# Windowed and pooled attention with a dense layer behind it: the first two dense tiles move into the banks that pair 0 leaves, with the planner's tables set anew

## The chip, the core and the metric

The kernel runs on one core of a Trainium2 chip. The core has a matrix engine (TensorE, PE in the profile), three engines for elementwise work (VectorE or DVE, ScalarE or ACT, GpSimd or POOL) and SyncE (SP), which issues the DMAs. Each engine works through its own queue in order and waits for others by semaphores. The metric is the device time of one execution in microseconds; the median of eight runs stands for a kernel.

## What is computed

Attention in two forms over q, k and v of 8 batches, 8 heads, 576 positions and 64 channels, and a dense layer on their sum:

```python
q_d, k_d, v_d = mean of 4 neighbouring positions of q, k, v
out_up = np.repeat(softmax(q_d k_d.T / 8) v_d, 4, axis=positions)
mask = np.abs(pos[:, None] - pos[None, :]) < 4
out_local = softmax(where(mask, q k.T / 8, -1e9)) v
x = (out_up + out_local)            # 4608 tokens x 512
h = x @ w_in                        # 512 x 2048
out = (h - np.tanh(h)) @ w_out      # 2048 x 512
```

## The kernel before

**Units.** Two heads are a pair (32 pairs), two pairs a group (16 groups), four pairs a batch. For a group, q and k come in by DMA as float32 (`qkn`), are cast and sorted to bfloat16 (`reorder`, L491), transposed by TensorE (`turn`, L520) and copied from PSUM into `qk` in two halves or as a whole (L529). Two adds (L533 into `half`, L538 into `qkd`) make the pooled q and k. v is cast (`prep_v`, L443), and its pooled form made by TensorE (`pool_v`, L462 and L464) and copied out (L469).

**A pair** (`attention`): scores of four windows (L587, for the first four pairs on top of a bias matmul, L581), their exponential (L623), the fifth window and the pooled scores (L587, L606) with theirs (L649, L652), the products with v (L669, L675), a reciprocal (L686), the normalisation into `ln` (L688), and the way back to channels on partitions. That way is either transposes (L744 to L748) with a copy `od` (L751) and an add (L754), or, for pairs in the table `UP`, "up" matmuls that add the repeated pooled part in PSUM (L723, L728) with one or two copies into `xT` (L734). From pair 12 on it is a DMA transpose.

**Dense layer.** The tokens are taken in 9 blocks of 512. `mm1` makes one tile of h (128 features by 512 tokens) from four matmuls, one for each chunk of 128 input channels. Chunk j is the `xT` of pair j of the batch, so block 0 needs pairs 0 to 3. Then come tanh on ScalarE (L786) and the subtraction on VectorE (L789); `mm2` makes the output from 16 matmuls for each 128 tokens. These 1,152 matmuls, 128x512, are most of TensorE's work, and are put between the steps of later pairs.

**PSUM.** There are eight banks. `ps_ts` and `ps_ox` (two banks each) serve attention throughout. `ps_ts1` and `ps_ox1` serve pairs 0 and 2 of the first batch only (pair 2 has its outputs in `ps_ts1`). Then `dense_banks` closes their pool and opens one of four dense banks, `ps_hy`. Tiles 0 to 3 of `mm1` therefore list both old names, "ts1" and "ox1", as written: they come after everything in these banks.

**Order.** The order is not written out. Steps are recorded with an engine (or a list of engines to choose from), a cost in ns, what they read and write, and a priority. `Program.order` then plays a greedy schedule through: on every engine the ready step of smallest priority goes first, and of steps with a choice the engine that is free first takes it. What comes out is each engine's fixed queue. Where the plan leaves TensorE idle before the dense layer, `emit` puts in filler matmuls (L1064). Tables give single steps their choice: `RE`, `RS` (sort), `TU`, `TS` (copies after the transposes; `TS` parts them in two halves), `AD`, `AS` (the adds; `AS` parts them), `CV` (v casts), `VD` (pooled v), `UP`, `PV` and `PLACE` (when a step is recorded), `URG` and `LATE` (priorities).

**What the steps of the prediction touch.** In the first 30 us: group 0's q and k (L491, L529, L533, L538), the pooled v of groups 0 and 1 (L469), the outputs and `ln` of pairs 0 to 3, their `xT` copies (L734), the casts of w_in (L434), and the first `mm1` tiles (L777). Later: pair 6's way back, and group 5's copies near 75 us.

Of the kernel before, what the change touches and what calls it, by code (L numbers as in the profile page):

```python
# [8 lines left out]
FP32 = mybir.dt.float32  # L9
# [3 lines left out]
PSUM = bass.MemoryType.PSUM  # L13


class Program:
# [147 lines left out]
def kernel(  # L164
# [26 lines left out]
    N_DC = Dm // 128  # L191
# [28 lines left out]
    vd = fixed("vd", [128, 2, 4, 65], BF16, NVW)  # L220
# [8 lines left out]
    od = fixed("od", [128, G], BF16, 2)  # L229
# [33 lines left out]
    op = P.op  # L263
# [497 lines left out]
    hy = [0]  # L761
    un = [0]

    def mm1(kb, fc):
        slot, us, g = hy[0] % 4, un[0] % 3, kb % 2
        hy[0] += 1
        un[0] += 1
        bs = sorted({kb * 512 // S, (kb * 512 + 511) // S})

        cut = 3 if kb == 0 and fc < 4 else 2  # L770
        old = ["ts1", "ox1"] if kb == 0 and fc < 4 else []

        def mm(part):
            if not ps_hy:
                dense_banks()
            for dc in range(cut) if part == 0 else range(cut, N_DC):
                T.matmul(ps_hy[slot], w_in_sb[:, dc, fc * 128:(fc + 1) * 128],  # L777
                         xT[dc][:, kb * 512:kb * 512 + 512],
                         start=(dc == 0), stop=(dc == N_DC - 1))
        for part in range(2):  # L780
            dcs = range(cut) if part == 0 else range(cut, N_DC)
            op("PE", 216 * len(dcs), lambda part=part: mm(part),
               reads=[("w_in", fc // 4, c) for c in dcs] +
               [(name, b, j) for b in bs for j in dcs for name in ("x", "xh")],
               writes=[("hy", slot)] + old, pri=P_A if old and part == 0 else 5000)
# [65 lines left out]
    def dense(kb):  # L851
# [18 lines left out]
        if kb == NBLK:  # L870
# [14 lines left out]
    T_QK, T_V, T_W, W_PRI = 900, 780, 2750, 53  # L885
    CAST = [("POOL", 620, GP.tensor_copy), ("ACT", 620, A.copy),
# [4 lines left out]
    CV = {0: 3, 1: 0, 2: 0, 3: 3, 4: 0, 5: 0, 6: 3, 7: 1, 8: 2, 9: 0, 10: 1, 11: 3}  # L891
# [4 lines left out]
    RE = {(0, 0): 0, (0, 1): 0, (1, 0): 1, (1, 1): 1, (2, 0): 1, (2, 1): 0, (3, 0): 3, (3,  # L896
          1): 0, (4, 0): 2, (4, 1): 1, (5, 0): 0, (5, 1): 0}
# [3 lines left out]
    TU = {(0, 0): 0, (0, 1): 0, (1, 0): 2, (1, 1): 2, (2, 0): 0, (2, 1): 0, (3, 0): 2, (3,  # L901
          1): 0, (4, 0): 0, (4, 1): 1, (5, 0): 1, (5, 1): 0}
# [12 lines left out]
    half_v, half_p = ("DVE", 420, 260, V), ("POOL", 650, 500, GP)  # L915
# [7 lines left out]
    URG = {'e1': {4: -2, 5: -2, 6: -2, 7: -2, 8: -2, 9: -2, 10: -2, 11: -2}, 'e2': {0: -2,  # L923
          1: -2, 2: -2, 3: -2, 4: -2, 5: -2, 6: -2, 7: -2, 8: -2, 9: -2, 10: -2, 11: -2},
          'norm': {0: -2, 1: -2, 2: -2, 3: -2, 4: -2, 5: -2, 6: -2, 7: -2}, 'add': {0: -2,
          1: -2}, 'turn': {4: -2, 5: -2}, 'vd': {4: -2, 5: -2}}
    ADDERS = [[("DVE", 760, 440, V), ("POOL", 1190, 850, GP)],
              [("POOL", 1190, 880, GP)], [("DVE", 760, 440, V)]]
    AD = {(0, 0): 1, (0, 1): 0, (1, 0): 0, (1, 1): 1, (2, 0): 1, (2, 1): 0, (3, 0): 0, (3,
          1): 1, (4, 0): 0, (4, 1): 0, (5, 0): 0, (5, 1): 2}  # L930
# [8 lines left out]
    for i in range(2):  # L939
        def guards(i=i):  # L940
# [3 lines left out]
           writes=[("qk", i, a, y) for a in range(2) for y in range(2)])  # L944
    for i in range(NVW):
        def ones(i=i):
# [3 lines left out]
           writes=[("vd", i), ("vw", i, 0), ("vw", i, 1)])  # L950
# [3 lines left out]
           writes=[("vd", i)], pri=-96)  # L954
# [141 lines left out]
```

The softmax here doesn't subtract the row's maximum and nothing guards it: scores larger than these inputs give would overflow.

## Time and profile before

| | us |
|---|---|
| median of 8 runs (lowest, highest) | 335.48 (334.74, 336.36) |
| the profiled execution | 335.51 |
| its span, first to last instruction | 333.8 |
| TensorE busy | 319.9 |
| VectorE, ScalarE, GpSimd busy | 236.5, 209.6, 155.5 |
| dense matmuls of line 777, mean of one | 0.379 |
| normalisation (L688), mean of one | 1.089 |
| granted TensorE clock over the span | 0.999 |

The profile is one execution. A matmul's busy time includes its passage through the array, so that following matmuls overlap: dense ones start every 0.215 us, although one lasts 0.379. A line of the timeline gives start, length, engine, source line, operation, output and inputs, shapes, count, and in brackets how long the engine had been idle and who ended that.

### The profile page before, as it was taken

How to read it: one execution, taken by the hardware profiler on the slowest of the kernel's cores; microseconds unless marked ns; L12 is line 12 of the kernel's file. 1: busy time of each engine (PE TensorE's matmuls, PEld its weight loads, DVE VectorE, ACT ScalarE, POOL GpSimd, SP SyncE). 2: the span in 40 equal slices, each digit the busy share in tenths (PEclk: the TensorE clock that was granted, in tenths of full speed). 3: DMA queues.
4: the chain of work that ended last, by engine and by line, in shares of the span. 5: the costliest groups of instructions: out<-in, count | busy, mean ns of one | idle time of the engine just before them, and what ended most of it. 6: DMA issues, size and time to landing. Idle time of an engine off the chain costs nothing.

```text
span 333.8 us, 6822 instructions
## 1 busy us (share of the span) xinstructions
PE 319.9 (96%) x2563; PEld 168.4 (50%) x2606; DVE 236.5 (71%) x386; ACT 209.6 (63%) x338; POOL 155.5 (47%) x183
## 2 busy tenths in 40 slices
PE   8778999999999999999999999999999999999996
PEld 5454555655554555554445444444444444444444
DVE  3697988789998879989687878787666443343300
ACT  1775877768858577668878786976654444444411
POOL 8673766249699488793939385652000000000000
PEclk9999999999999999999999999999999999999999
DMA  6999999999993889799899889843233000100012
GB/s 207 253 380 322 301 269 355 241 247 278 308 262 88 218 208 278 200 224 253 227 248 265 212 238 190 164 98 89 59 76 73 33 31 31 63 33 31 31 70 90
DMA packets 96878, 60.47 MB, mean 181 GB/s; under 512 B 74510, under 2 KB 80078, under 8 KB 96846
## 3 DMA queue, kind: packets, MB, share of 16 engines
q1 hardware_dynamic: 96846, 60.04, 67.0%
q8 instruction: 20, 0.33, 0.4%
q14 instruction: 12, 0.10, 0.1%
HBM read 43.05 MB, written 9.44 MB: 157 GB/s over the span
## 4 chain that ended last, share of the span: by engine, by line
PE 82%; DVE 9%; issue 4%; POOL 3%; ACT 1%; POOLq 0%; DVEq 0%; ACTq 0%
PE ps_hy L777 35%; PE ps_hy L832 34%; PE ps_ts L587 3%; PE ps_ox L669 3%; PE ps_ox L675 2%; DVE ln L688 2%; PE ps_ts L520 1%; DVE qk L529 1%; PE ps_hy L807 1%; DVE half L533 1%; DVE qr L491 1%; DVE E L656 1%; DVE gT L789 1%; DVE E L627 1%; DVE qkd L538 1%
## 5 line engine op out<-in xcount | busy, mean ns | idle before, releaser
L777 PE MATMUL ps_hy<-xT,w_in_sb 128*128 128x512 bf16 x553 | 141.8, 379 | 2.2 <-issue 1.1
L832 PE MATMUL ps_hy<-w_out_sb,gT 128*128 128x512 bf16 x540 | 137.2, 379 | 1.4 <-issue 0.5
L789 DVE TENSOR_TENSOR gT<-ps_hy,uy 128x512 bf16<-128x512 f32 x144 | 95.2, 685 | 57.9 <-ACT uy L786 56.1
L786 ACT ACTIVATE uy<-ps_hy 128x512 f32<-128x512 f32 x144 | 83.4, 601 | 61.6 <-PE ps_hy L777 57.3
L777 PEld LDWEIGHTS <-w_in_sb 128*128 128x128 bf16 x576 | 53.1, 98 | 59.3 <-issue 1.0
L832 PEld LDWEIGHTS <-gT 128*128 128x128 bf16 x560 | 52.3, 98 | 58.1
L533 POOL TENSOR_TENSOR half<-qk 128x576 f32<-128x576 bf16 (+1 forms) x33 | 34.9, 1061 | 39.1 <-ACT qk L529 34.6
L688 DVE TENSOR_TENSOR ln<-ps_ox,r 128x896 bf16<-128x896 f32 x30 | 32.7, 1089 | 0.8
L623 ACT ACTIVATE E<-ps_ts 128x960 bf16<-128x960 f32 x30 | 29.4, 981 | 2.1 <-PE ps_ts L587 2.1
L843 ACT COPY uy<-ps_hy 128x512 f32<-128x512 f32 x35 | 20.6, 589 | 14.3 <-PE ps_hy L832 12.6
L443 POOL CAST vw<-vst 128x640 bf16<-128x640 f32 x27 | 24.2, 900 | 10.7 <-DMA vst<-in_v_dram 7.3
L708 DVE TENSOR_TENSOR xT<-lnT 128x480 bf16<-128x480 bf16 (+1 forms) x40 | 28.2, 721 | 0.0
L356 POOL TENSOR_TENSOR qkn<-qkn 128x512 f32<-128x512 f32 (+1 forms) x18 | 25.1, 1397 | 4.9 <-DMA qkn<-in_v_dram 4.2
L529 ACT COPY qk<-ps_ts 128x1152 bf16<-128x1152 bf16 (+1 forms) x16 | 16.1, 1004 | 17.3 <-DVE qk L529 6.6
L627 DVE TENSOR_TENSOR E<-E,mask 128x960 bf16<-128x960 bf16 x28 | 23.3, 831 | 4.4 <-ACT E L623 4.4
L538 POOL TENSOR_TENSOR qkd<-half 128x288 bf16<-128x288 f32 (+1 forms) x31 | 20.9, 677 | 4.0 <-DVE half L533 2.7
L529 ACT COPY qk<-vst 128x1152 bf16<-128x1152 bf16 x10 | 22.1, 2209 | 0.9 <-POOL half L533 0.7
L491 DVE CAST qr<-qkn 128x1152 bf16<-128x1152 f32 (+1 forms) x18 | 17.8, 988 | 3.8 <-DMA qkn<-in_q_dram 2.3
L491 POOL CAST qr<-qkn 128x1152 bf16<-128x1152 f32 (+1 forms) x14 | 17.0, 1217 | 6.2 <-DMA qkn<-in_k_dram 3.2
L669 PEld LDWEIGHTS <-E 128*128 128x128 bf16 x300 | 15.3, 98 | 7.3 <-issue 0.6
L669 PE MATMUL ps_ox<-vw,E 128*128 128x65 bf16 x300 | 18.2, 194 | 0.5 <-DVE xT L734 0.3
L587 PEld LDWEIGHTS <-qk 64*128 64x128 bf16 x320 | 9.5, 95 | 17.6 <-issue 15.6
(107 smaller groups left out, 295.6 us busy)
## 6 DMA issues: line engine op xcount, KB each, us to landing
vst<-in_v_dram SPq DMA_DIRECT2D x62, 160.0 KB, 4.9
qkn<-in_q_dram SPq DMA_DIRECT2D x32, 288.0 KB, 4.3
qkn<-in_k_dram SPq DMA_DIRECT2D x32, 288.0 KB, 5.0
out_dram<-uy SPq DMA_DIRECT2D x35, 256.0 KB, 3.6
qkn<-in_v_dram SPq DMA_DIRECT2D x9, 512.0 KB, 5.1
gT<-in_moe_w_in_dram SPq DMA_DIRECT2D x4, 1024.0 KB, 9.2
xT<-in_moe_w_out_dram SPq DMA_DIRECT2D x8, 256.0 KB, 4.9
gT<-in_moe_w_out_dram SPq DMA_DIRECT2D x2, 1024.0 KB, 7.5
```

The costliest lines, as they stand in the source:

```text
L491: P.choice([(eng, ns, lambda fn=fn, x0=x0, x1=x1: fn(out=dst[:, x0:x1], in_=srt[:, x0:x1])) for eng, ns, fn in table], reads=[("qkn", sn, ...
L529: fn(out=o[:, ys].rearrange("p y (g a) -> p y g a", a=A6), in_=b16.rearrange("p (a g y) -> p y g a", a=A6, y=2)[:, ys])
L533: eng.tensor_tensor(out=half[:, ys], in0=four[:, ys, :, 0:2], in1=four[:, ys, :, 2:4], op=ALU.add)
L623: op("ACT", 980, lambda: A.activation(out=e1, in_=ps[:, :, 0:480], func=AF.Exp, scale=SCALE), reads=ts, writes=[("E", se, 0)], pri=URG.get ...
L627: op("DVE", 900, lambda: V.tensor_tensor(out=e1, in0=e1, in1=mask[:, 0:480].unsqueeze(1).to_broadcast([128, 2, 480]), op=ALU.mult), reads= ...
L669: T.matmul(po[:, hh, 65 * t:65 * t + 65], E[se][:, c:c + 128], vw[w][:, 2 * jj + hh, t, :], start=True, stop=True)
L688: op("DVE", 1090, lambda: V.tensor_tensor(out=ln[sl].rearrange("p n (h d) -> p h n d", d=D), in0=blocks[:, :, :, 0:64], in1=r[s].unsqueeze ...
L708: up=up: eng.tensor_tensor(out=xo[:, QW * t0:QW * t0 + nt * n].rearrange("p (t g a) -> p t g a", t=nt, a=4), in0=lnT[sl][:, t0:t0 + nt, 0: ...
L777: T.matmul(ps_hy[slot], w_in_sb[:, dc, fc * 128:(fc + 1) * 128], xT[dc][:, kb * 512:kb * 512 + 512], start=(dc == 0), stop=(dc == N_DC - 1))
L786: op("ACT", 490, lambda: A.activation(out=u[us], in_=ps_hy[slot], func=AF.Tanh), reads=[("hy", slot)], writes=[("u", us)], pri=-1)
L789: op("DVE", 620, lambda: V.tensor_tensor(out=gT[g][:, fc, :], in0=ps_hy[slot], in1=u[us], op=ALU.subtract), reads=[("hy", slot), ("u", us) ...
L832: T.matmul(ps_hy[slot], gT[g][:, fc, ts * 128:ts * 128 + 128], w_out_sb[:, fc, :], start=(fc == 0), stop=(fc == N_FF - 1))
```

## The change

The pool of `ps_ts1` and `ps_ox1` becomes two pools, one bank pair each, and `dense_banks(slot)` closes them one by one: first `ps_ox1` for dense banks 0 and 1, then `ps_ts1` for 2 and 3. Tiles 0 and 1 of `mm1` list only "ox1", tiles 2 and 3 only "ts1". Tiles 0 and 1 are recorded in three parts (chunks 0 and 1; 2; 3), tiles 2 and 3 in two (chunks 0 to 2; 3). The tables get new values.

```diff
-    early = ExitStack()
-    psum_e = early.enter_context(tc.tile_pool(name="psum_e", bufs=1, space=PSUM))
-    ps_ts1 = fixed("ps_ts1", [128, 2, 512], FP32, pool=psum_e)
-    ps_ox1 = fixed("ps_ox1", [128, 2, 512], FP32, pool=psum_e)
-
-    def dense_banks():
-        early.close()
-        pool = ctx.enter_context(tc.tile_pool(name="psum_d", bufs=1, space=PSUM))
-        ps_hy.extend(fixed("ps_hy", [128, 512], FP32, 4, pool=pool))
+    early = [ExitStack() for _ in range(2)]
+    pools = [s.enter_context(tc.tile_pool(name=f"psum_e{i}", bufs=1, space=PSUM,
+                                            side=("left", "right")[i]))
+             for i, s in enumerate(early)]
+    ps_ts1 = fixed("ps_ts1", [128, 2, 512], FP32, pool=pools[0])
+    ps_ox1 = fixed("ps_ox1", [128, 2, 512], FP32, pool=pools[1])
+    def dense_banks(slot):
+        while slot >= len(ps_hy):
+            i = len(ps_hy)
+            early.pop().close()
+            pool = ctx.enter_context(tc.tile_pool(name=f"psum_d{i}", bufs=1, space=PSUM,
+                                                  side=("right", "left")[i // 2]))
+            ps_hy.extend(fixed(f"ps_hy{i}", [128, 512], FP32, 2, pool=pool))
...
-        cut = 3 if kb == 0 and fc < 4 else 2
-        old = ["ts1", "ox1"] if kb == 0 and fc < 4 else []
+        old, parts = [], (range(0, 2), range(2, 4))
+        if kb == 0 and fc < 4:
+            old = ["ox1"] if fc < 2 else ["ts1"]
+            parts = (range(0, 2), range(2, 3), range(3, 4)) if fc < 2 else (range(3), range(3, 4))
...
-               writes=[("hy", slot)] + old, pri=P_A if old and part == 0 else 5000)
+               writes=[("hy", slot)] + old, pri=P_A if old and dcs[-1] < 3 else 5000)
...
-    P_A, LATE = 5000, {0: 25, 2: 40, 3: 40}
+    P_A, LATE = 5000, {0: 40, 2: 40, 3: 40}
...
-    PV = {2: 0, 3: 0, 4: -1, 5: -1, 6: 0}
-    PLACE = {2: (1, 3), 3: (1, 2), 4: (4, 4), 5: (1, 2), 6: (4, 4), 7: (1, 1), 8: (3, 3)}
+    PV = {2: 0, 3: 1, 4: -1, 5: 0, 6: 1}
+    PLACE = {2: (0, 2), 3: (1, 2), 4: (4, 4), 5: (1, 2), 6: (4, 4), 7: (1, 1), 8: (3, 3)}
...
-    PV1 = True
-    VD = {0: 1, 1: 2, 2: 1, 3: 0, 4: 1, 5: 0, 6: 1}
-    RS = {(0, 1): 2, (1, 0): 4, (1, 1): 1}
-    UP = {0: 0, 1: 0, 2: 0, 3: 3, 4: 3, 8: 0, 11: 3}
+    PV1 = False
+    VD = {0: 2, 1: 0, 2: 1, 3: 1, 4: 1, 5: 0, 6: 1}
+    RS = {(0, 1): 2, (1, 0): 4, (1, 1): 3, (3, 0): 4}
+    UP = {0: 3, 1: 0, 2: 3, 3: 3, 4: 2, 6: 3, 8: 1, 11: 3}
...
-    TS = {(0, 0): 1, (0, 1): 2, (1, 1): 2, (2, 1): 2, (4, 0): 2, (5, 0): 2, (5, 1): 1}
-    AS = {(1, 0): 2, (1, 1): 1, (2, 0): 1, (2, 1): 1, (5, 0): 1, (5, 1): 4, (6, 1): 1}
+    TS = {(0, 0): 1, (0, 1): 2, (1, 1): 2, (2, 1): 2, (5, 0): 1, (5, 1): 3}
+    AS = {(0, 0): 1, (1, 0): 1, (1, 1): 1, (2, 0): 1, (4, 0): 1, (5, 0): 4, (5, 1): 4, (6,
+          1): 1}
...
-          'norm': {0: -2, 1: -2, 2: -2, 3: -2, 4: -2, 5: -2, 6: -2, 7: -2}, 'add': {0: -2,
-          1: -2}, 'turn': {4: -2, 5: -2}, 'vd': {4: -2, 5: -2}}
+          5: -2, 6: -2, 7: -2, 8: -2, 9: -2, 10: -2, 11: -2}, 'od': {0: -2, 1: -2}, 'norm':
+          {0: -2, 1: -2, 2: -2, 3: -2, 4: -2, 5: -2, 6: -2, 7: -2, 8: -2, 9: -2, 10: -2, 11:
+          -2}, 'add': {0: -2, 1: -2, 2: -2, 3: -2, 4: -2, 5: -2, 6: -2, 7: -2}, 'turn': {4:
+          -2, 5: -2}, 'vd': {2: -2, 3: -2}}
```

CV, RE, TU and AD also change, for groups up to 5 (CV up to pair 11). `PV1` moves the pooled v of pairs 2 and 3 (group 1) from `ps_ts1` to `ps_ox`.

More of the change, by code (lines that the diff above doesn't have):

```diff
@@ L768, in mm1, with mm @@
         bs = sorted({kb * 512 // S, (kb * 512 + 511) // S})
-        cut = 3 if kb == 0 and fc < 4 else 2
-        old = ["ts1", "ox1"] if kb == 0 and fc < 4 else []
[L773 to L776, printed above, removed]
+        old, parts = [], (range(0, 2), range(2, 4))
+        if kb == 0 and fc < 4:
+            old = ["ox1"] if fc < 2 else ["ts1"]
+            parts = (range(0, 2), range(2, 3), range(3, 4)) if fc < 2 else (range(3), range(3, 4))
+        def mm(dcs):
+            dense_banks(slot)
+            for dc in dcs:
                 T.matmul(ps_hy[slot], w_in_sb[:, dc, fc * 128:(fc + 1) * 128],
@@ L779, in mm @@
                          start=(dc == 0), stop=(dc == N_DC - 1))
-        for part in range(2):
-            dcs = range(cut) if part == 0 else range(cut, N_DC)
-            op("PE", 216 * len(dcs), lambda part=part: mm(part),
+        for dcs in parts:
+            op("PE", 216 * len(dcs), lambda dcs=dcs: mm(dcs),
                reads=[("w_in", fc // 4, c) for c in dcs] +
                [(name, b, j) for b in bs for j in dcs for name in ("x", "xh")],
-               writes=[("hy", slot)] + old, pri=P_A if old and part == 0 else 5000)
+               writes=[("hy", slot)] + old, pri=P_A if old and dcs[-1] < 3 else 5000)
         op("ACT", 490, lambda: A.activation(
@@ L890 @@
               [("DVE", 500, V.tensor_copy)]]
[L891 removed]
+    CV = {0: 3, 1: 1, 2: 1, 3: 3, 4: 1, 5: 0, 6: 3, 7: 0, 8: 2, 9: 0, 10: 2, 11: 3}
     REORDER = [[("DVE", 860, V.tensor_copy), ("ACT", 950, A.copy),
@@ L895 @@
                [("DVE", 1150, V.tensor_copy)], [("POOL", 1350, GP.tensor_copy)]]
-    RE = {(0, 0): 0, (0, 1): 0, (1, 0): 1, (1, 1): 1, (2, 0): 1, (2, 1): 0, (3, 0): 3, (3,
-          1): 0, (4, 0): 2, (4, 1): 1, (5, 0): 0, (5, 1): 0}
+    RE = {(0, 0): 1, (0, 1): 4, (1, 0): 2, (1, 1): 4, (2, 0): 3, (2, 1): 4, (3, 0): 0, (3,
+          1): 0, (4, 0): 2, (4, 1): 4, (5, 0): 1, (5, 1): 1}
     TURN = [[("ACT", 1125, A.copy), ("DVE", 1250, V.tensor_copy)],
@@ L900 @@
             [("ACT", 2210, A.copy)]]
-    TU = {(0, 0): 0, (0, 1): 0, (1, 0): 2, (1, 1): 2, (2, 0): 0, (2, 1): 0, (3, 0): 2, (3,
-          1): 0, (4, 0): 0, (4, 1): 1, (5, 0): 1, (5, 1): 0}
+    TU = {(0, 0): 2, (0, 1): 1, (1, 0): 2, (1, 1): 1, (2, 0): 1, (2, 1): 1, (3, 0): 2, (3,
+          1): 1, (4, 0): 1, (4, 1): 1, (5, 0): 1, (5, 1): 1}
     re_v, re_a, re_p = (("DVE", 480, V.tensor_copy), ("ACT", 580, A.copy),
@@ L920 @@
              [[half_p], [half_p]]]
-    TS = {(0, 0): 1, (0, 1): 2, (1, 1): 2, (2, 1): 2, (4, 0): 2, (5, 0): 2, (5, 1): 1}
-    AS = {(1, 0): 2, (1, 1): 1, (2, 0): 1, (2, 1): 1, (5, 0): 1, (5, 1): 4, (6, 1): 1}
-    URG = {'e1': {4: -2, 5: -2, 6: -2, 7: -2, 8: -2, 9: -2, 10: -2, 11: -2}, 'e2': {0: -2,
-          1: -2, 2: -2, 3: -2, 4: -2, 5: -2, 6: -2, 7: -2, 8: -2, 9: -2, 10: -2, 11: -2},
-          'norm': {0: -2, 1: -2, 2: -2, 3: -2, 4: -2, 5: -2, 6: -2, 7: -2}, 'add': {0: -2,
-          1: -2}, 'turn': {4: -2, 5: -2}, 'vd': {4: -2, 5: -2}}
+    TS = {(0, 0): 1, (0, 1): 2, (1, 1): 2, (2, 1): 2, (5, 0): 1, (5, 1): 3}
+    AS = {(0, 0): 1, (1, 0): 1, (1, 1): 1, (2, 0): 1, (4, 0): 1, (5, 0): 4, (5, 1): 4, (6,
+          1): 1}
+    URG = {'e1': {8: -2, 9: -2, 10: -2, 11: -2}, 'e2': {0: -2, 1: -2, 2: -2, 3: -2, 4: -2,
+          5: -2, 6: -2, 7: -2, 8: -2, 9: -2, 10: -2, 11: -2}, 'od': {0: -2, 1: -2}, 'norm':
+          {0: -2, 1: -2, 2: -2, 3: -2, 4: -2, 5: -2, 6: -2, 7: -2, 8: -2, 9: -2, 10: -2, 11:
+          -2}, 'add': {0: -2, 1: -2, 2: -2, 3: -2, 4: -2, 5: -2, 6: -2, 7: -2}, 'turn': {4:
+          -2, 5: -2}, 'vd': {2: -2, 3: -2}}
     ADDERS = [[("DVE", 760, 440, V), ("POOL", 1190, 850, GP)],
               [("POOL", 1190, 880, GP)], [("DVE", 760, 440, V)]]
-    AD = {(0, 0): 1, (0, 1): 0, (1, 0): 0, (1, 1): 1, (2, 0): 1, (2, 1): 0, (3, 0): 0, (3,
-          1): 1, (4, 0): 0, (4, 1): 0, (5, 0): 0, (5, 1): 2}
+    AD = {(0, 0): 2, (0, 1): 2, (1, 0): 0, (1, 1): 1, (2, 0): 0, (2, 1): 1, (3, 0): 0, (3,
+          1): 1, (4, 0): 0, (4, 1): 0, (5, 0): 2, (5, 1): 1}
     op("DVE", 180, lambda: V.memset(warm, 0.0), writes=["warm"], pri=-999)
```

## Prediction

> **What bounds the kernel now.** The first view is the page: engine totals and slices.
>
> ```profile
> span 333.8 us, 6822 instructions
> ...
> PE 319.9 (96%) x2563; PEld 168.4 (50%) x2606; DVE 236.5 (71%) x386; ACT 209.6 (63%) x338; POOL 155.5 (47%) x183
> ...
> PE   8778999999999999999999999999999999999996
> ```
>
> TensorE is full from the fifth slice on, about 30 us, when the dense layers begin. From there to the end it issues a fixed list of matmuls, so the end lies where the dense start puts it, plus TensorE's waits after it. The start is read in TensorE's own timeline:
>
> ```profile
> 25.74 0.84 PE L1064 MATMUL ps_ox<-warm 128*128 128x320 bf16 x5
> 26.84 0.30 PE L723 MATMUL ps_ts<-spread,ln 128*128 128x288 bf16 x1 [0.26 <-DVE ln L688]
> ...
> 27.36 0.43 PE L1064 MATMUL ps_ox<-warm 128*128 128x320 bf16 x2
> 28.11 0.30 PE L723 MATMUL ps_ts<-spread,ln 128*128 128x288 bf16 x1 [0.32 <-DVE ln L688]
> ...
> 28.64 0.81 PE L777 MATMUL ps_hy<-xT,w_in_sb 128*128 128x512 bf16 x2
> 29.78 4.69 PE L777 MATMUL ps_hy<-xT,w_in_sb 128*128 128x512 bf16 x21 [0.33 <-DVE xT L734]
> ```
>
> TensorE waits for VectorE's normalised ln (L688); fillers (L1064) sit in those waits. Three chunks of dense tile 0 run at 28.6, and the fourth waits until 29.78 for xT of pair 3. After 30 us the weight loads (all recorded; some matmuls are not) show four waits: 0.45 us at 52.6, 0.96 at 97.8, 0.4 at 100.2, 0.35 at 138.4.
>
> VectorE's timeline at the start, then one line each from GpSimd's and ScalarE's:
>
> ```profile
> 7.83 0.76 DVE L529 COPY qk<-ps_ts 128x576 bf16<-128x576 bf16 x1 [1.98 <-PE ps_ts L520]
> 8.51 0.74 DVE L491 CAST qr<-qkn 128x576 bf16<-128x576 f32 x1
> 11.98 0.76 DVE L529 COPY qk<-ps_ts 128x576 bf16<-128x576 bf16 x1 [2.73 <-ACT qk L529]
> 12.84 1.00 DVE L533 TENSOR_TENSOR half<-qk 128x576 f32<-128x576 bf16 x1
> ```
> ```profile
> 8.49 1.66 POOL L317 TENSOR_SCALAR mask<-bias 128x576 bf16<-128x576 bf16 x1
> ```
> ```profile
> 8.62 0.64 ACT L529 COPY qk<-ps_ts 128x576 bf16<-128x576 bf16 x1 [6.55 <-DVE qk L529]
> ```
>
> The point is the 8.51 line: VectorE sorts its half of group 0's k straight after its copy of q; TensorE's k transposes follow at 10.4.
>
> **The change, part by part.** I read the changed order on each engine; durations are the trace's.
>
> *Dense tiles ahead.* The ox1 banks come free when pair 0's xT is copied, the ts1 banks still after pair 2's. In the new TensorE order two chunks of tile 0 stand before pair 3's up-matmuls, then chunk 2 of tile 0 and three chunks of tile 2, then the chunk that needs pair 3. So six dense matmuls instead of three are done when it comes: 3 x 0.215 us (spacing of these matmuls) = **-0.65 us**. Four of the seven late fillers go; they sat in waits, so that is worth nothing.
>
> *AS (0,0).* Today GpSimd does both adds of group 0's q (10.12 to 12.0). In the new order VectorE takes one half (add to half, add to qkd), and both stand **ahead of its sort of k**. The first add waits for ScalarE's copy, which ends at 9.26: 9.31 to 9.77 (0.46, the 128x288 add at 36.16). GpSimd's add of the other half follows (0.66), VectorE's second add gets through after it, near 10.55, and the sort after GpSimd's second add, 10.5 to 11.5. So TensorE's k transposes move from 10.4 to about 11.55: +1.15. Everything queued behind them (scores of pairs 0 and 1, the exponentials, group 1) moves along. Some returns: the 12.84 add took 1.00 us against 0.76 alone (63.83), as a GpSimd cast ran until 13.23; that cast is now over before. **+0.8 is left** at pair 2's second scores (20.3).
>
> Here a rule weighs in. "SBUF — State Buffer", section "Who interferes with whom", in the Trainium skill says that VectorE instructions with two SBUF inputs share a port with GpSimd, and that whoever comes first holds it for the whole instruction. The 12.84 row agrees. Taken strictly, the mask on GpSimd (8.49 to 10.15) would hold back the moved add until 10.15 and k's transposes to about 12.1 (+1.7). The row says less: the mask took 1.66 us while VectorE's cast ran beside it for 0.74, so it may itself be the one that waited, and alone end at 9.4. I take the row (+1.15); the rule adds 0.5 to the upper end. Below nothing it can't go: k's sort can't start earlier than today.
>
> *VD and LATE.* The pooled v of pairs 0 and 1 (vd0) leaves PSUM on VectorE (0.68) instead of ScalarE, behind its qkd adds, so it ends about 0.3 later still; pair 0's outputs go first and need it. Outputs 20.54 -> 21.6, first reciprocal 21.32 -> 22.4 (**+1.1** in all).
>
> *UP, VD and the w_in casts in VectorE's chain.* Today from first reciprocal to last ln: 21.32 to 28.06 = 6.74 us: four steps of 1.27, the vd1 cast 0.68, xT0 0.76, small gaps. New: four steps; two w_in casts (0.42 each at 27.97) right after the first ln, in a stretch where GpSimd casts too (up to +0.5); half of xT0 (0.46), which now waits for ScalarE's half, some 0.35; vd1 goes to ScalarE. 5.1 + 0.84 + 0.46 + 0.35 + 0.4 = 7.15, **+0.4**. The last ln ends at 29.6 instead of 28.06. Pair 3's up-matmuls and the two xT copies then run as today (1.6 us): the chunk that needs pair 3 comes at 31.3 instead of 29.78, +1.5. With the 0.65 ahead: **+0.85 us** at the dense start. The other retargeted steps before 30 us (w_in halves, vw casts) are at nothing: loads have landed before they are reached, and SyncE's order of DMAs does not change. If they collided they would add 0.2 to 0.4 on VectorE.
>
> *UP adds pair 6.* Its transposes back (0.37 us of issue, from 55.73) become up-matmuls (0.53, from 22.82): **+0.16**, TensorE being full there; it saves 0.3 to 0.75 us on ScalarE and VectorE, which do not bound.
>
> *TS and AS for group 5, near 75 us.* Today: TensorE's second transposes of group 5 at 72.9, VectorE's copy 73.70 to 74.45, ScalarE's 74.48 to 75.12; under these stand eight dense matmuls and six of scores, and the outputs (L669, same bank ps_ox) follow without a wait. New: before the outputs stand only eight score matmuls and four dense ones, 1.4 us with the slow entry of the scores. On ScalarE two tanh (1.1), then its copy (0.64), then VectorE's copy (0.75), which waits for it: about 2.7 us after the transposes. **+1.2** of wait; bounds 0 (both tanh done before) and +1.5. Nothing beside TensorE hides it; it is in order.
>
> *The other tables* (RE, TU, AD, PV, CV, URG to group 6) move casts and copies among engines that are 47 to 71% busy. They may lengthen or remove the four waits (2.2 us in sum) and add others: bounds -1.5 and +1.0, taken at 0, since the trace has no row for orders that never ran.
>
> Sum: 0.85 + 0.16 + 1.2 = **+2.2 us**. The profiled execution took 335.51 us (span 333.8 and 1.7 around it) and the median is 335.48, the same: **337.7 us**.
>
> **The rivals.**
> - *The early tiles pay* (other side). Place: the k sort. If TensorE's k transposes slip under 0.3 us, because VectorE's first add falls into its idle time before 11.98 and nothing behind feels it, the last ln is no later and the 0.65 us is kept; with the wait at 97.8 shortened (more 'add' and 'norm' at urgent priority) up to 1.4 goes: 333.9 to 334.8. It decides once the delay of the last ln is below 0.65. For it: VectorE was idle 2.7 us there. Against: the sort stands behind the adds in a queue in order. 0.14.
> - *Start lost, group 5 hidden.* ScalarE reaches both tanh early: +1.0, 336.5 (335.9 to 337.0). For it: the same transposes cost nothing today. 0.22.
> - *The port rule in full, and new waits in 50 to 110 us.* +0.5 and +1.0 on top: 339.2. For it: GpSimd and VectorE overlap at all these places. 0.12.
> - *A wash:* dense start +0.85 less, waits -1: 335.5. 0.09.
> - The change does not do what it says: excluded, the new order shows the tiles ahead.
>
> **How the numbers follow.** My forecast (337.0 to 338.7) has 0.43, the rivals 0.14, 0.22, 0.12, 0.09. About 0.2% (0.67 us) is what a measurement here can tell from no change. Faster 0.14; same 0.10 (the wash and a bit of its neighbours); slower 0.76. The range 335.1 to 339.8 leaves out most of the first rival and the tail of the third.
>
> **What would show it.** k's transposes of group 0 near 11.5 with a wait on VectorE; the first reciprocal near 22.4; pair 3's up-matmuls near 29.7; six dense matmuls before the chunk that waits; a wait of about 1 us before outputs near 76 us. The prediction is wrong if the last ln of the first four pairs ends before 28.7, or if waits after 31 us sum to under 2 us.

## The result, and the profile after

| | before | after |
|---|---|---|
| median, us (lowest to highest; runs) | 335.49 (334.56 to 338.16; 32) | 337.51 (336.94 to 338.89; 11) |
| ratio after to before (95% interval) | | 1.0056 (1.0038 to 1.0074) |
| profiled execution, us | 335.51 | 337.32 |
| its span, us | 333.8 | 335.6 |
| granted TensorE clock over the span | 0.999 | 1.000 |

The change costs 2.0 us. Forecast were 2.2. Medians and ratios here and below leave out one execution of before (340.44 us) and the profiled one of tiles_late (476.49 us at a granted clock of 0.657), so that no trace of tiles_late is read. Behind the code of the banks all lines are numbered three to five higher than before (L777 is now L781, L669 is L672), and in the kernels of the experiments up to fifteen. From the page of after, totals and slices of TensorE:

```profile
span 335.6 us, 6819 instructions
...
PE 319.5 (95%) x2560; PEld 167.8 (50%) x2602; DVE 236.7 (71%) x388; ACT 211.0 (63%) x341; POOL 152.7 (46%) x181
...
PE   8778999989998999999999999999999999999996
```

TensorE is as busy as before (319.5 us against 319.9) in a longer span, so the loss is waiting. The ninth and the thirteenth slice, from 67 and from 101 us, now show an 8 where before has a 9.

**The start.** TensorE's timeline of before (group 0's transposes of q and of k), then that of after (the same, the first dense matmuls, the up-matmuls of pair 3), then VectorE's and GpSimd's of after:

```profile
7.13 0.67 PE L520 MATMUL ps_ts<-ident,qr 128*128 128x128 bf16 x9
...
10.41 0.67 PE L520 MATMUL ps_ts<-ident,qr 128*128 128x128 bf16 x9
```
```profile
6.61 0.67 PE L523 MATMUL ps_ts<-ident,qr 128*128 128x128 bf16 x9
...
10.61 0.66 PE L523 MATMUL ps_ts<-ident,qr 128*128 128x128 bf16 x9 [0.55 <-DVE qr L494]
...
27.60 0.60 PE L781 MATMUL ps_hy<-xT,w_in_sb 128*128 128x512 bf16 x2
28.42 0.30 PE L726 MATMUL ps_ts<-spread,ln 128*128 128x288 bf16 x1 [0.23 <-DVE ln L691]
```
```profile
8.78 0.68 DVE L536 TENSOR_TENSOR half<-qk 128x288 f32<-128x288 bf16 x1 [0.70 <-ACT qk L532]
9.49 0.31 DVE L541 TENSOR_TENSOR qkd<-half 128x144 bf16<-128x144 f32 x1
9.72 0.75 DVE L494 CAST qr<-qkn 128x576 bf16<-128x576 f32 x1
11.98 0.76 DVE L532 COPY qk<-ps_ts 128x576 bf16<-128x576 bf16 x1 [1.52 <-ACT qk L532]
```
```profile
8.48 1.66 POOL L320 TENSOR_SCALAR mask<-bias 128x576 bf16<-128x576 bf16 x1
10.12 0.67 POOL L536 TENSOR_TENSOR half<-qk 128x288 f32<-128x288 bf16 x1
```

The two adds do stand ahead of the sort of k, and TensorE waits for that sort. But two executions can't be compared by their clock here: group 0's *first* transposes, which the change doesn't touch, start at 7.13 us before and at 6.61 after. In the profiles below they start anywhere from 6.6 to 8.0, and I call this time the opening. So I count from these first transposes:

| us after the first transposes | before | after | forecast step | measured step |
|---|---|---|---|---|
| k's transposes | 3.28 | 4.00 | +1.15 | +0.72 |
| pair 3's up-matmuls | 20.98 | 21.81 | +1.5 | +0.83 |
| the chunk that needs pair 3 | 22.65 | 23.48 | +1.5 | +0.83 |

Six dense matmuls instead of three are done when that chunk comes, as forecast, worth 0.65. The dense start lost 0.18 us, not 0.85. Even this count is not free of the opening: g5_copy_first (experiment 3) has the order of after up to 70 us and an opening of 7.21, near that of before. There the three steps are +0.50, +0.60 and +0.60, and nothing is lost at the dense start (-0.05).

**Later.** I count a wait as the time between two weight loads (all recorded) beyond what the same two lines usually take, where this is over 0.2 us. From 31 us on, before has 2.45 us of it and after 4.46: 0.42 at 51.4, 0.30 at 73.1, 1.30 at 75.4, 0.33 at 82.9, 0.85 at 97.4, 0.51 at 101.7, 0.40 at 102.5 and 0.35 at 140.6 us. A wait right behind a dense matmul (75.4 and 97.4, in before 53.1) holds some 0.19 us of that matmul; without these the sums are 2.3 and 4.1. The largest, in the timelines of TensorE, ScalarE and VectorE of after, and then the same place in before:

```profile
72.23 0.67 PE L523 MATMUL ps_ox<-ident,qr 128*128 128x128 bf16 x9
73.13 0.39 PE L590 MATMUL ps_ts<-qk 64*128 64x120 bf16 x8 [0.23 <-ACT qk L532]
73.67 0.81 PE L781 MATMUL ps_hy<-xT,w_in_sb 128*128 128x512 bf16 x3 [0.16 <-issue]
75.44 0.32 PE L672 MATMUL ps_ox<-vw,E 128*128 128x65 bf16 x5 [0.95 <-DVE qk L532]
```
```profile
72.44 0.64 ACT L532 COPY qk<-ps_ts 128x576 bf16<-128x576 bf16 x1 [0.78 <-DVE qk L532]
72.97 1.09 ACT L789 ACTIVATE uy<-ps_hy 128x512 f32<-128x512 f32 x2
73.94 0.66 ACT L532 COPY qk<-ps_ox 128x576 bf16<-128x576 bf16 x1
```
```profile
74.63 0.76 DVE L532 COPY qk<-ps_ox 128x576 bf16<-128x576 bf16 x1 [1.56 <-ACT qk L532]
```
```profile
75.52 0.32 PE L669 MATMUL ps_ox<-vw,E 128*128 128x65 bf16 x5
```
```profile
74.48 0.64 ACT L529 COPY qk<-ps_ox 128x576 bf16<-128x576 bf16 x1 [0.34 <-DVE qk L529]
```
```profile
73.70 0.75 DVE L529 COPY qk<-ps_ox 128x576 bf16<-128x576 bf16 x1
```

In after, group 5's copy on ScalarE stands behind two tanh, VectorE's half waits for it, and the outputs of pair 8 wait for that, as the prediction drew it. In before, VectorE's half comes first and the outputs do not wait.

**Where the loss lies by equal work.** At the outputs of pair 12 both kernels have done the same matmuls (140 of h, 78 of the output product). At those of pair 7 they differ by two dense ones, which after has still to do. TensorE's timelines, of before and of after:

```profile
65.57 0.32 PE L669 MATMUL ps_ox<-vw,E 128*128 128x65 bf16 x5
...
103.05 0.32 PE L669 MATMUL ps_ox<-vw,E 128*128 128x65 bf16 x5
```
```profile
65.00 0.32 PE L672 MATMUL ps_ox<-vw,E 128*128 128x65 bf16 x5
...
104.88 0.32 PE L672 MATMUL ps_ox<-vw,E 128*128 128x65 bf16 x5
```

Between them lie 37.48 us before and 39.88 after: 2.4 us, 0.43 of them the two matmuls. From there to the end both take 230.7 us. So nearly the whole loss falls between 65 and 105 us.

### The profile page after: what moved, and what is told of

Same layout as the page of the kernel before. It is cut to its first block, busy times and chain, and to the rows that moved or that the text cites. A ratio compares the mean times of both kernels' runs of the same rounds, so it can differ in the third digit from the quotient of the medians.

```text
span 335.6 us, 6819 instructions
## 1 busy us (share of the span) xinstructions
PE 319.5 (95%) x2560; PEld 167.8 (50%) x2602; DVE 236.7 (71%) x388; ACT 211.0 (63%) x341; POOL 152.7 (46%) x181
## 4 chain that ended last, share of the span: by engine, by line
PE 80%; DVE 10%; issue 3%; POOL 3%; DMA 2%; ACT 2%; SPq 0%; POOLq 0%; DVEq 0%; ACTq 0%
PE ps_hy L835 33%; PE ps_hy L781 32%; PE ps_ts L590 2%; PE ps_ox L672 2%; DVE ln L691 2%; DMA vst<-in_v_dram 2%; PE ps_ts L523 2%; PE ps_ox L678 2%; PE ps_ts L1069 2%; DVE qk L532 2%; ACT qk L532 1%; DVE gT L792 1%; POOL half L536 1%; PE ps_hy L810 1%; DVE half L536 1%
## 5 line engine op out<-in xcount | busy, mean ns | idle before, releaser
L781 PE MATMUL ps_hy<-xT,w_in_sb 128*128 128x512 bf16 x555 | 141.9, 379 | 2.0 <-issue 1.0
L781 PEld LDWEIGHTS <-w_in_sb 128*128 128x128 bf16 x576 | 53.1, 98 | 60.0 <-issue 1.2
L536 POOL TENSOR_TENSOR half<-qk 128x576 f32<-128x576 bf16 (+1 forms) x32 | 32.6, 1021 | 44.9 <-ACT qk L532 36.0
L630 DVE TENSOR_TENSOR E<-E,mask 128x960 bf16<-128x960 bf16 x28 | 25.4, 906 | 5.0 <-ACT E L626 4.9
L359 POOL TENSOR_TENSOR qkn<-qkn 128x512 f32<-128x512 f32 (+1 forms) x18 | 25.9, 1438 | 3.2 <-DMA qkn<-in_v_dram 2.5
L446 POOL CAST vw<-vst 128x640 bf16<-128x640 f32 x26 | 22.2, 856 | 7.9 <-DMA vst<-in_v_dram 7.9
L494 POOL CAST qr<-qkn 128x1152 bf16<-128x1152 f32 (+1 forms) x16 | 18.8, 1179 | 9.4 <-DMA qkn<-in_k_dram 4.6
L541 POOL TENSOR_TENSOR qkd<-half 128x288 bf16<-128x288 f32 (+1 forms) x32 | 21.7, 682 | 1.6 <-DVE half L536 0.4
L672 PE MATMUL ps_ox<-vw,E 128*128 128x65 bf16 x300 | 18.2, 194 | 1.9 <-DVE qk L532 1.0
L672 PEld LDWEIGHTS <-E 128*128 128x128 bf16 x300 | 15.4, 98 | 8.9 <-issue 2.3
L678 PE MATMUL ps_ox<-vd,E 128*128 128x65 bf16 x240 | 16.9, 192 | 0.0
```

The costliest lines, as they stand in the source:

```text
L359: op("POOL", 1330, lambda t=t: GP.tensor_tensor(out=t[:, :, 0:2], in0=t[:, :, 0:2], in1=t[:, :, 2:4], op=ALU.add), writes=keys, pri=pri)
L536: eng.tensor_tensor(out=half[:, ys], in0=four[:, ys, :, 0:2], in1=four[:, ys, :, 2:4], op=ALU.add)
L630: op("DVE", 900, lambda: V.tensor_tensor(out=e1, in0=e1, in1=mask[:, 0:480].unsqueeze(1).to_broadcast([128, 2, 480]), op=ALU.mult), reads= ...
L672: T.matmul(po[:, hh, 65 * t:65 * t + 65], E[se][:, c:c + 128], vw[w][:, 2 * jj + hh, t, :], start=True, stop=True)
```

## Experiments

Each ran against the kernel before. Ahead of each stands what was expected: a theory, and a rival, the other explanation that the run could show. "Plan held" means that the order planned for the base kernel is used on every engine, and only the named steps are moved in it. Without that, the schedule is made anew for every edit.

**1 and 2. The banks alone, the tables alone.** *banks_only* is before with the new code of the banks and the parts of `mm1`; *tables_only* is after with the old code. Both are planned anew.

```diff
-        cut = 3 if kb == 0 and fc < 4 else 2
-        old = ["ts1", "ox1"] if kb == 0 and fc < 4 else []
+        old, parts = [], (range(0, 2), range(2, 4))
+        if kb == 0 and fc < 4:
+            old = ["ox1"] if fc < 2 else ["ts1"]
...
```

> The kernel before with only the new bank and part code (two pools, tiles 0 and 1 in three parts); all tables as before. Theory (the tiles pay and the tables cost): VectorE's and ScalarE's queues are those of before until 30 us, so the last ln ends where it did (28.0 to 28.1 us), six or more dense matmuls instead of three stand ahead of the chunk that needs pair 3, and the dense start gains 0.65 us; the plan behind it is made anew, with waits after 31 us of about 2 us as before: 334.5 to 335.2 us. Rival (the tiles' gain is given back, and the loss of the change sits in the bank code): 335.5 us or more, with the 0.65 us gone again before 60 us. If the total is over 336, the planner's new order behind the start costs by itself, and the waits after 31 us will show it.

> The changed kernel with the bank and part code of before (one pool, tiles 0 to 3 wait for both bank pairs); all tables as changed. Theory: the loss is in the tables; no early tiles, so the chunk that needs pair 3 has three dense matmuls ahead instead of six, 0.65 us more than the changed kernel: 337.8 to 338.6 us. Rival (the bank code carries the loss): 335.5 us or below.

Measured: banks_only 337.46 us, ratio 1.0064 (1.0042 to 1.0086); tables_only 337.63, ratio 1.0057 (1.0036 to 1.0077). Each half alone costs what the whole costs. My theory on banks_only falls: the new tables are not needed for the loss. From 73 us on its waits are nearly those of after, the largest at the same place (TensorE's timeline of banks_only):

```profile
75.56 0.32 PE L672 MATMUL ps_ox<-vw,E 128*128 128x65 bf16 x5 [1.38 <-DVE qk L532]
```

This kernel has the *old* `TS` and `AS` of group 5. So the wait that the prediction put down to their new values also comes without them, from the plan that is made anew once the dense tiles can begin earlier. *tables_only* came out just under its theory (337.8 to 338.6), and not with the same waits: at 75 us nothing waits for group 5, but 0.96 us stand at 73.3 for an exponential on ScalarE, 0.47 at 74.4 for an add into xT, and 0.88 at 144.5 (TensorE's timeline of tables_only):

```profile
73.28 0.66 PE L520 MATMUL ps_ts<-ident,qr 128*128 128x128 bf16 x9 [0.96 <-ACT E L652]
```

Its loss was not followed further.

**3. Group 5's copy ahead of the two tanh** (after, plan held).

```diff
+PIN = [(546, 478)]
...
+        for i, j in PIN:
+            order.remove(i)
+            order.insert(order.index(j), i)
         for i in order:
```

> The changed kernel with one step moved: ScalarE's copy of its half of group 5's second transposes goes ahead of the two tanh at 73.0 us; every other order is held as it is. Theory: the copy starts at about 73.1 instead of 73.94, VectorE's half follows at 73.8 instead of 74.63, and the outputs of pair 8 come 0.8 us earlier, so the wait of 0.95 us before them falls to about 0.15: 0.8 us less, 336.7 us. Rival: the tanh are needed as soon, their dense banks come free 0.65 us later, and the wait moves to a dense matmul that needs the bank: 337.3 to 337.5 us.

Measured: 337.39 us, ratio 1.0054 (1.0035 to 1.0073). The rival holds: the total is that of after, though two such medians are uncertain against each other by some 0.9 us, so that a small gain can't be told. The wait before the outputs of pair 8 shrank from 1.30 to 0.32 us, and 0.91 us stood up at 80.5, for another reason than I had named (TensorE's, then ScalarE's timeline of g5_copy_first):

```profile
80.52 1.02 PE L787 MATMUL ps_hy<-xT,w_in_sb 128*128 128x512 bf16 x4 [0.75 <-ACT uy L852]
```
```profile
79.88 0.59 ACT L852 COPY uy<-ps_hy 128x512 f32<-128x512 f32 x1 [1.06 <-DMA out_dram<-uy]
```

ScalarE could not copy the fourth output tile, as the DMA that empties its buffer had not landed. ScalarE had begun to write that DMA's data at 59.6 us (0.6 us), but the DMA was issued at 75.0, behind 15 us of loads in SyncE's queue.

**4. The adds of group 0's q back on GpSimd** (after, plan held).

```diff
+PIN = [(104, 103), (105, 106)]
...
+            P.swap = {at + 2: ("POOL", 650, lambda: add1(GP, each[1][0])),
+                      at + 3: ("POOL", 500, lambda: add2(GP, each[1][0]))}
```

> The changed kernel with VectorE's two adds of group 0's q (the half that AS (0,0) put there) back on GpSimd; every other order held. Theory of the prediction (the adds hold up the k sort, and through it everything to the dense start): VectorE sorts k at 8.1 instead of 9.7, k's transposes come 0.5 to 0.8 us earlier than 10.6, and 0.5 us is left at the last ln and in the total: 337.0 us. Rival (the adds are hidden, as ScalarE's half of the k sort ends hardly earlier, or what is gained is taken back by GpSimd's later pooled q): k's transposes 0 to 0.6 us earlier, last ln within 0.2 us of 28.36, total 337.3 to 337.7.

Measured: 337.71 us, ratio 1.0064 (1.0041 to 1.0087). At k's transposes the theory holds: they come 3.29 us after the first ones, as before (4.00 in after). Pair 3's up-matmuls come 21.09 us after the first transposes (21.81 in after), but that is not what the adds are worth. The opening of this execution is late (8.00 us, against 6.61). Two other kernels tell more, as they have like openings and in the first 65 us differ in nothing but these adds: three_undone (experiment 11) has them on GpSimd, g5_copy_first has them on VectorE. TensorE's timelines of three_undone and of g5_copy_first:

```profile
7.14 0.67 PE L528 MATMUL ps_ts<-ident,qr 128*128 128x128 bf16 x9
...
28.69 0.30 PE L735 MATMUL ps_ts<-spread,ln 128*128 128x288 bf16 x1 [0.23 <-DVE ln L700]
```
```profile
7.21 0.67 PE L529 MATMUL ps_ts<-ident,qr 128*128 128x128 bf16 x9
...
28.79 0.30 PE L732 MATMUL ps_ts<-spread,ln 128*128 128x288 bf16 x1 [0.23 <-DVE ln L697]
```

The steps are 21.55 and 21.58 us: of the 0.5 us that k gains, 0.03 is left at pair 3. The total shows no gain either, but its uncertainty against after is about 1 us, so that it alone could not exclude the 0.5 us of the theory.

**5 to 7. The early matmuls by themselves, plan held.** In *before_early3* two chunks of tile 0 take the place of two fillers, and three of tile 2 go ahead of the chunk that needs pair 3. *before_early8* moves two chunks each of tiles 0 and 1 to an earlier place, that of five fillers ahead of pair 2's up-matmuls, and chunk 2 of both and three of tile 2 ahead of the chunk that needs pair 3. *tiles_late* puts the early matmuls of after back behind the steps that they had overtaken. From the edit of before_early3:

```diff
+LEAD = {229: [(0, (0, 1))], 249: [(2, (0, 1, 2))]}
...
+            for fc, dcs in LEAD.get(i, ()):
+                self.tiles[fc](0, dcs)
```

> The kernel before with the new banks, and its plan held on every engine but for five dense matmuls: chunks 0 and 1 of tile 0 take the place of two fillers ahead of pair 3's up-matmuls, and three chunks of tile 2 go ahead of the chunk that needs pair 3. So six dense matmuls stand ahead of that chunk instead of three, and nothing else moves. Theory (the early tiles themselves are worth their 0.65 us, and what the bank code costs by itself is the plan that is made anew behind it): the wait before the chunk shrinks, 0.65 us less in all, 334.7 to 335.0 us, with the waits after 31 us as before (2.3 us). Rival (the gain is absorbed, since a later stretch, 72 to 102 us, is set by VectorE, GpSimd or the DMAs and not by TensorE): the waits after 31 us grow by 0.5 to 0.65 us and the total stays at 335.4.

> As before_early3, but with more: chunks 0 and 1 of tiles 0 and 1 take the place of the five fillers ahead of pair 2's up-matmuls, and behind pair 3's up-matmuls come chunk 2 of both tiles and three chunks of tile 2. Nine dense matmuls instead of three stand ahead of the chunk that needs pair 3, about as many as fit. Theory: 6 x 0.215 = 1.3 us less, 334.1 to 334.4 us. Rival (absorbed between 72 and 102 us): waits after 31 us larger by 1 us or more, 335.2 or above.

> The changed kernel with its plan held, but the early dense matmuls put back: tile 0's first two chunks behind pair 3's up-matmuls, and tile 2's first three chunks behind the chunk that needs pair 3. Theory (each early matmul is worth its time): 0.65 us more than the changed kernel, 338.1 us, with the wait of 0.95 us before the outputs of pair 8 unchanged, since the steps it waits for follow TensorE. Rival (absorbed): that wait, or the ones at 96 to 102 us, shrink by as much and the total stays at 337.5.

Measured: before_early3 335.22 us, ratio 0.9998 (0.9986 to 1.0009); before_early8 334.97, 0.9990 (0.9977 to 1.0003); tiles_late 338.53, 1.0092 (1.0074 to 1.0110; four executions). In after's plan the early matmuls are thus worth something: by the two ratios 1.2 us, uncertain by some 0.8. In before's plan nothing or little of them is left: the 0.65 and 1.3 us of the theories lie outside the intervals. But nothing is lost either, and this settles the cause: before_early3 has the new banks of banks_only in the order planned for before, and costs nothing, while banks_only with its new order costs 2.0 us. It is the order made anew that costs, not the banks and not the early tiles. The six matmuls of before_early3 are done in time, and then (VectorE's and TensorE's timelines of before_early3)

```profile
33.10 1.46 DVE L500 CAST qr<-qkn 128x1152 bf16<-128x1152 f32 x1
```
```profile
34.62 0.68 PE L529 MATMUL ps_ox<-ident,qr 128*128 128x128 bf16 x9 [0.69 <-DVE qr L500]
```

Group 2's transposes wait for VectorE's sort of q, behind three subtractions and beside a sort on GpSimd (32.80 to 33.95 us). It was the same rival as I had named (absorbed), but at 34 us and not at 72 to 102.

**8. Fewer fillers at the opening** (before, plan held: 22 instead of 29).

> The kernel before with 22 instead of 29 filler matmuls at the very start, nothing else. In six profiles so far group 0's first transposes started anywhere from 6.6 to 8.0 us, always right after the last of the 29 fillers, which took 5.3 to 6.7 us of weight-load time, while the sort of q that they need had ended at 5.7 to 6.5. Theory (this is where the spread of about 1 us between executions comes from, and the fillers hold up the start): first transposes at 6.0 to 6.7 us, 0.5 to 1 us less in all, 334.5 to 335.0. Rival (fewer fillers leave TensorE's clock low for the transposes and scores behind, or the group's later steps wait for loads): no gain, or 335.5 to 336.5.

Measured: 335.53 us, ratio 0.9998 (0.9985 to 1.0011): no gain. In the profiled execution the fillers end early, and the sort is late instead (VectorE's and TensorE's timelines of before_fill22):

```profile
5.97 1.31 DVE L493 CAST qr<-qkn 128x1152 bf16<-128x1152 f32 x1 [3.21 <-DMA qkn<-in_q_dram]
```
```profile
7.34 0.68 PE L522 MATMUL ps_ts<-ident,qr 128*128 128x128 bf16 x9 [1.55 <-DVE qr L493]
```

Two things end close together at the opening: the fillers and the first load with its sort. Taking one away shows the other. In the other profiles this sort starts at 4.9 to 5.7 us and takes 0.8, so that one trace does not show that the sort is in the way in most executions.

**9. The output DMA earlier as well** (g5_copy_first, and in SyncE's queue the DMA ahead of six loads).

```diff
+        for i, j in [(546, 478), (468, 588), (470, 588), (472, 588), (474, 588), (584, 588), (586, 588)]:
...
```

> g5_copy_first with one more step moved: the DMA that takes the first 128 output tokens to DRAM stands in SyncE's queue behind 15 us of loads, although its data is ready at 59.6 us; here it goes ahead of the four v loads and the two q loads before it (issue near 69.5 instead of 75.0 us). In g5_copy_first ScalarE's fourth output copy waited 1.06 us for that DMA to free its buffer, and a dense matmul 0.75 us behind it at 80.5. Theory (group 5's wait was only moved to this DMA, and both cover one real loss): no wait at 80.5, and the total falls by 0.8 us against g5_copy_first, 336.6 us. Rival (the stretch from 75 to 90 us is set by VectorE, busy 2.97 to 3.00 of every 3 us there): a new wait of 0.5 us or more on VectorE between 76 and 92 us, total 337.2 to 337.5.

Measured: 337.50 us, ratio 1.0066 (1.0042 to 1.0091). The wait at 80.5 is gone, and 0.32 at 82.6 and 0.43 at 86.8 us have come: in sum what the rival expected, in two pieces.

**10. The early tiles and the wait at 34 us** (before_early3, and tile 6 ahead of group 2's transposes).

> before_early3 with four more dense matmuls moved: tile 6 goes ahead of group 2's first transposes, where TensorE waited 1.06 us at 34.6 us for VectorE's sort of q. Theory (the early tiles' 0.65 us was absorbed at this one place, because an in-order queue had the transposes next): the wait falls to 0.2 us or less, and 0.65 us is kept: 334.6 to 334.9 us. Rival (the elementwise engines set the pace from 33 to 45 us, so that TensorE waits at the next step): new waits of 0.5 us or more before 50 us, total 335.2.

Measured: 335.27 us, ratio 0.9996 (0.9985 to 1.0006). The wait at 34.6 is gone; 0.67 us at 36.5 and 0.46 at 39.4 have come: the rival.

**11. Three waits of after taken away together** (plan held; the adds of experiment 4 are moved by the same code as there).

```diff
...
+        for i, j in [(546, 478), (468, 588), (470, 588), (472, 588), (474, 588), (584, 588), (586, 588), (623, 646), (104, 103), (105, 106)]:
...
```

> The changed kernel with three things put right in its own plan: the adds of group 0's q on GpSimd (as in q_adds_pool), group 5's copy and the output DMA earlier (as in g5_out_first), and the add into xT of pair 10 on VectorE ahead of the add into half that took 1.36 us at 95.3 us beside GpSimd's sort (0.46 alone), since the outputs of pair 11 waited 0.85 us behind both. Theory (these waits are the loss, and they add up): the stretch from the outputs of pair 7 to those of pair 12 takes 38.5 us or less instead of 39.9 (37.5 in the kernel before), and the total is 336.0 to 336.4. Rival (this stretch is paced by VectorE and GpSimd together in the changed order of work, so that each wait taken away comes back behind): 39.3 us or more for the stretch, 336.9 to 337.3 in all.

Measured: 336.96 us, ratio 1.0059 (1.0037 to 1.0081), the stretch from pair 7 to pair 12 39.31 us: the rival's numbers. Between 74 and 101 us TensorE then waits only 0.32 us, and after that (TensorE's, ScalarE's and GpSimd's timelines of three_undone)

```profile
101.49 0.22 PE L599 MATMUL ps_ts<-qk 64*128 64x96 bf16 x2 [1.70 <-ACT qk L537]
```
```profile
100.31 1.12 ACT L537 COPY qk<-ps_ts 128x1152 bf16<-128x1152 bf16 x1 [3.48 <-POOL half L541]
```
```profile
97.12 1.46 POOL L451 CAST vw<-vst 128x640 bf16<-128x640 f32 x2
98.54 1.74 POOL L541 TENSOR_TENSOR half<-qk 128x576 f32<-128x576 bf16 x1
```

TensorE waits for a copy, the copy for an add on GpSimd that reads the same `qk`, and that add stands in a queue with hardly a gap from 93 us on. Busy time by stretch, first of before, then of after (the length of the stretch, then busy us and number of instructions of PE, PEld, DVE, ACT and POOL, then granted clock, DMA share and GB/s):

```profile
72.00:76.00 4.00, 3.79 (x49) 2.20 (x49) 3.96 (x7) 3.66 (x8) 1.94 (x2) 1.00 1.15 263
76.00:84.00 8.00, 7.95 (x86) 3.93 (x84) 7.57 (x12) 6.91 (x13) 7.63 (x12) 1.00 0.96 263
84.00:93.00 9.00, 8.79 (x89) 5.53 (x92) 8.67 (x16) 7.88 (x15) 6.58 (x7) 1.00 1.09 308
93.00:102.00 9.00, 7.82 (x80) 4.68 (x78) 8.97 (x13) 4.50 (x8) 8.92 (x10) 1.00 0.83 235
```
```profile
72.00:76.00 4.00, 2.66 (x40) 1.86 (x40) 2.44 (x5) 3.52 (x6) 2.30 (x3) 1.00 1.04 246
76.00:84.00 8.00, 7.78 (x82) 3.83 (x80) 7.93 (x12) 6.26 (x13) 6.50 (x11) 1.00 1.06 285
84.00:93.00 9.00, 8.89 (x82) 5.33 (x83) 8.32 (x16) 7.86 (x14) 4.73 (x5) 1.00 1.10 306
93.00:102.00 9.00, 8.01 (x86) 4.68 (x86) 7.64 (x11) 4.57 (x7) 8.84 (x10) 1.00 0.79 230
```

Before keeps VectorE working at 72 to 76 us (3.96 of 4), after lets it stand for 1.56 us behind group 5's copy. From 76 to 93 us GpSimd does 14.21 us of work before (7.63 and 6.58) and 11.23 after (6.50 and 4.73), since among other gaps it stands for 3.13 us ahead of an add (at 92.56) that needs a copy of the next group's transposes (ScalarE, 91.29 to 92.41); from 93 on it is full in both. Time that VectorE or GpSimd lose ahead of the place where they are full isn't had back there, and which of TensorE's steps shows the wait is secondary. That GpSimd's queue at 93 to 103 us took back what three_undone had won is read from its trace (there it does 12.63 us of work from 76 to 93 us); that it is also what sets after itself is argued from these rows, and no run took work from GpSimd there.

**12. A version that beats both** (before_early8, plan held, and two pairs of dense matmuls ahead of steps that TensorE waited for).

```diff
+        for i, j in [(315, 390), (670, 777)]:
```

> before_early8 with two pairs of dense matmuls moved ahead of steps that TensorE waited for: two of the output product ahead of the outputs of pair 5 (0.44 us of wait at 53.3 us) and two of h ahead of the pooled v of group 6 (0.44 us at 100.1). Nothing else moves. Theory (before 65 us TensorE's order is what loses time, not the other engines): both waits go to 0.05 us or less, and 0.8 us is gained against before_early8: 334.2 us. Rival (the other engines set the pace there too): new waits of 0.3 us or more behind each, 334.8 to 335.3.

Measured: 334.74 us, ratio 0.9980 (0.9966 to 0.9993): 0.6 us faster than before, of 1.2 hoped for. Against before_early8 it is 0.2 us, less than the noise, and near the rival's 334.8 to 335.3. The outputs of pair 5 no longer wait 0.44 us; 0.45 us stands up at 55.1, and 0.29 at 99.3 in place of 0.44 at 100.1.

## Why the prediction was right, point by point

The total was right, 337.7 against 337.51, but that it came so close was luck: two errors of size stood against each other. The shares, from the profiles: dense start +0.18, or -0.05 in g5_copy_first (forecast +0.85); pair 6 +0.16 (not measured by itself); waits after 31 us +1.8 to +2.0 (forecast +1.2). Together about +2.2; after's first transposes came 0.52 us early in its profiled execution, which leaves 1.7. The spans differ by 1.8.

- *Early tiles, -0.65:* six matmuls ahead, as forecast. Of the late fillers two are left (at 22.35 in after), not three of seven; they sit in waits all the same.
- *AS (0,0), +1.15 at k, +0.8 left at pair 2's second scores:* the right place and sign at k, +0.72 measured (+0.50 in g5_copy_first), and q_adds_pool shows that these adds are the cause there. The term was too large because I let GpSimd's add of the other half come between VectorE's two adds (second add "near 10.55"). GpSimd's add had to wait for the mask and began at 10.12; VectorE's second add took 0.31 us at 9.49, and the sort was over before GpSimd's second. What is left was worse: pair 2's second scores moved by +0.28, and by +0.05 in g5_copy_first. VectorE stood idle for 2.73 us ahead of its copy at 11.98 in before and for 1.52 in after, so that most of the delay fell into idle time, and the next add took 0.76 us (12.85) instead of 1.00. That is the reasoning of the rival "the early tiles pay", which I had held to fail because the sort stands behind the adds.
- *The port rule weighed there* (the Trainium skill, "SBUF — State Buffer", "Who interferes with whom"), which taken strictly would hold VectorE's adds until the mask ends at 10.14, is not what happened: both adds ran under the mask, the first in 0.68 us instead of 0.46, the second in 0.31. In g5_copy_first they took 0.46 and 0.31 under it. With the rule the sum would have been too large by a further 0.5. My own reading, that VectorE had lengthened the mask, which would end at 9.4 alone, gets no support: beside quite other work it took 1.66 us again.
- *VD, LATE and VectorE's chain, +1.1 and +0.4:* the outputs did wait for VectorE's copy of the pooled v, by 0.30 us (TensorE's timeline of after):

```profile
20.66 0.32 PE L672 MATMUL ps_ox<-vw,E 128*128 128x65 bf16 x5 [0.30 <-DVE vd L472]
```

  Counted from the first transposes, the first reciprocal moved from 14.19 to 14.81, +0.62 (14.59 in g5_copy_first, +0.40); from there to the last ln went 6.74 to 6.94 us, +0.2. As the adds of q leave next to nothing there, this copy and this chain make most of the 0.6 us by which pair 3 is late; that is read from the traces, and no run moved the copy back.
- *The signs of being wrong:* the last ln was not to end before 28.7, and it ended at 28.36. By its own sign, then, the account of the start was wrong. A clock time of one execution was a bad sign to choose, but counted from the first transposes the last ln also moved by +0.82 only (+0.59 in g5_copy_first), not by +1.5. The other sign, waits after 31 us of under 2 us, did not occur; it could hardly, as before has 2.45 by the same count.
- *Group 5, +1.2:* the wait is there, 0.95 us before the outputs and 0.23 before the scores. But the step gave it to `TS` and `AS`, and banks_only has it with the old tables; and it was taken as a price that would be saved if it were gone, while g5_copy_first saved nothing that can be told. Place and size were right, the cause was not.
- *Other tables, 0 with bounds -1.5 and +1.0:* the waits outside group 5 grew by about 0.4 us. Here the reasoning had no hold: it took the plan behind the start as given, and only banks_only, beside before_early3, showed that a new order for the same banks is enough for the whole loss.

Of the rivals, "the early tiles pay" failed on something I had not considered. Its tiles do come early and are worth time in after's plan, and the delay of k is hidden as it said, but the steps behind cost more. "Start lost, group 5 hidden" failed, as group 5 was not hidden. "The port rule in full" failed at the mask. What stays open is which of the planner's many moved steps between 31 and 72 us brings the copies of group 5 and the transposes of the next group late; no run isolates one. Why the tables alone cost as much is open as well.

## What to carry to other kernels

When queues come from a scheduler, an edit to one place is an edit to all of them: hold the order and move single steps, or the experiment measures the scheduler. Compare two traces by the time at equal work and from a common event, not by their clocks: here the opening alone shifted by up to 1.4 us between executions. And choose executions that open alike, as an opening is not passed on in full: the same order needed 21.81 us to pair 3 with an opening of 6.61, and 21.58 with one of 7.21. A wait on the busiest engine is a saving only if no other queue is full behind it; nearly all that were taken away here came back in part or whole within 30 us.

## What was unexpected of the hardware

- GpSimd's mask (TENSOR_SCALAR) did not hold up VectorE's adds, whose inputs are both in SBUF. In g5_copy_first they took 0.46 and 0.31 us under it, which is what such adds take in after where they begin ahead of GpSimd's instruction (0.46 at 63.74) or beside none (0.30 at 19.71). VectorE's and GpSimd's timelines of g5_copy_first:

```profile
9.38 0.46 DVE L542 TENSOR_TENSOR half<-qk 128x288 f32<-128x288 bf16 x1 [0.70 <-ACT qk L538]
9.87 0.31 DVE L547 TENSOR_TENSOR qkd<-half 128x144 bf16<-128x144 f32 x1
```
```profile
8.37 1.67 POOL L326 TENSOR_SCALAR mask<-bias 128x576 bf16<-128x576 bf16 x1
```

  Other GpSimd work did. A 128x288 add on VectorE that takes 0.46 us (before's trace, 36.16) took 1.36 in after, beside a GpSimd cast (VectorE's and GpSimd's timelines of after):

```profile
95.28 1.36 DVE L536 TENSOR_TENSOR half<-qk 128x288 f32<-128x288 bf16 x1 [0.45 <-POOL qkd L541]
```
```profile
95.19 1.15 POOL L494 CAST qr<-qkn 128x1152 bf16<-128x1152 f32 x1
```

- The same 29 filler matmuls at the opening took from 5.6 us (after) to 7.0 (q_adds_pool), with no wait between them. By their weight loads they follow each other every 0.267 us at first and every 0.136 us later, and the change comes at 4.4 us in after, 5.5 in before and 7.3 in q_adds_pool. That moment makes the whole difference between these openings.
- In g5_copy_first an output DMA whose data was written from 59.6 us on was issued at 75.0 and landed at 79.9: 15 us were the queue of loads on SyncE, 4.9 the time from issue to landing.
